# K and v of ten tiles as seven block products per pair, in a kernel for linear attention and routed experts

## The chip, the cores and the metric

The kernel runs on one core of one Trainium2 chip. The metric is the device time of one launch in microseconds. Engines are called as the profile calls them: PE multiplies matrices, DVE, ACT and POOL work on tiles in SBUF (DVE and ACT also in PSUM, where PE's results land), SP starts most transfers. Each engine takes its instructions in the order in which the program lists them.

## The reference

A sequence of 2048 rows of 512 numbers goes through two branches, which are mixed row by row by a sigmoid gate.

```
g = sigmoid((x * gate_w).sum(-1))
# branch A: linear attention, 32 heads of 16
q, k, v = split(x @ wqkv)
phi(y)  = concat(softmax(y @ w_phi), softmax(-(y @ w_phi)))   # 32 features a head
kv = sum over rows of phi(k)^T v ;  z = sum over rows of phi(k)
a  = (phi(q) kv) / (phi(q) z + 1e-6) @ wo
# branch B: for each of 32 heads the best of 16 x 16 experts
s1, s2 = x @ w_q @ k1, x @ w_q @ k2 ;  e = 16 * argmax(s1) + argmax(s2)
b  = sum over heads of gelu(x . u[e]) * v[e]
out = g * a + (1 - g) * b
```

## The kernel before

The rows are cut into 16 tiles of 128 (`t`). Each tile lies transposed, as four blocks of 128 x 128 (`k` = 0 to 3). All products keep float32 accuracy by three matmuls: every operand is held as a high part (`xh`, `wah`, `wbh`) and a low part (`xl`, `wal`, `wbl`, the source less the high part), and `mm3` adds high x high, high x low and low x high. A projection of one tile on 512 columns (`proj`) is 4 x 3 = 12 matmuls of 128 x 512 into one PSUM bank. Four banks rotate under the name `mm`, three under `tr`, one (`acc`) holds the sums over rows.

The first stage, about 128 us, prepares weights and builds the sums over rows. Its loop over `t` does, for each tile:

- `x_load(t + 3)`: SP starts a load of 256 KB into one of three buffers (`xr`); `x_split` makes the high part on ACT and the low part on DVE (L132, L133).
- `vproj(t)` projects on v (weights `wbh`, `wbl`), and ACT copies the result into `vs[t]`. `kproj(t)` projects on k (weights `wah`, `wal`, with `w_phi` folded in), and DVE takes differences from each head's maximum and minimum (`softmax_diffs`, four instructions: the differences of tile t). Tiles 14 and 15 get their v much later.
- ACT takes the exponential (L346), `ksoft` the sums and reciprocals on DVE (L200, L201) and the product with them on POOL (L202). The text calls these exp(t), sum(t) and k_mult(t).
- Every second tile `kvacc` adds phi(k)^T v of two tiles: 32 small matmuls a tile. Ones in a 17th column of v give the sums z; for tiles 14 and 15 `kvz` makes them alone with 32 matmuls of one column.
- By the table `plan`, `score_w` multiplies a piece of `w_q` (1 MB, two buffers) with the keys. After two pieces, `score_planes(j)` copies the result to `wpl`, and SP starts a transpose by DMA into `wtp`; `score_join(j)` copies it back (`wtj`), splits it into `sh` on ACT and `sl` on POOL. `wpl`, `wtp` and `wtj` have one buffer each.

After the loop, `fold_q` folds `w_phi` into the query weights (`rawq`, loaded in the loop), `front_s` and the rest begin the second stage, a loop over the tiles for all that remains; there, in its second round, v of tiles 14 and 15 is projected.

Nothing is scheduled automatically: each engine's order is the order of these calls.

Of the kernel before, what the change touches and what calls it, by code (L numbers as in the profile page):

```python
# [20 lines left out]
P = 128  # L21
# [14 lines left out]
def mix_kernel(ctx, tc, xT, wqT, wkT, wv, wphi, wo, wq, kk, ug, ev, cst, out):  # L36
# [28 lines left out]
    xh = per.tile([P, NT, NK, P], F32R, name="xh")  # L65
    xl = per.tile([P, NT, NK, P], F32R, name="xl")
# [7 lines left out]
    wbl = per.tile([P, NK, D], F32R, name="wbl")  # L74
    uh = per.tile([P, NK, NW], F32R, name="uh")
# [8 lines left out]
    def xs(t, k):  # L84
        return xh[:, t, k, :], xl[:, t, k, :]
# [30 lines left out]
    warm = w1.tile([P, 384], BF16, bufs=1, name="warm")  # L116
# [8 lines left out]
    def x_load(t):  # L125
        r = rawx[t] = wa_.tile([P, NK, P], F32, tag="xr", bufs=3, name=f"xr{t}")
        if t > 0:
            sp.dma_start(r, xT[t])

    def x_split(t, ks=slice(0, NK)):  # L130
        r = rawx[t]
        (dve.tensor_copy if t < 3 else act.copy)(xh[:, t, ks], r[:, ks])  # L132
        dve.tensor_tensor(xl[:, t, ks], r[:, ks], xh[:, t, ks], op=ALU.subtract)  # L133
# [33 lines left out]
    def fold_turn(tmp, wh, wl):  # L167
# [6 lines left out]
        for k in range(NK):  # L174
            act.copy(by_head(wh[:, k]), by_row(o[k]))
            dve.tensor_tensor(by_head(wl[:, k]), by_row(o[k]), by_head(wh[:, k]), op=ALU.subtract)

    acc = psum.tile([P, 512], F32, tag="acc", name="kvacc")[:, :8 * (F + 1)].rearrange("p (g c) -> p g c", c=F + 1)
    phis, vs, pvs, wsP, stk, joins = {}, {}, {}, {}, {}, []

    def vproj(t, ks=range(NK)):
        if ks[0] > 0:
            return proj(pvs.pop(t), t, wbh, wbl, 0, D, ks)
        pv = pvs[t] = mm_bank(f"pv{t}")
        proj(pv, t, wbh, wbl, 0, D, ks)
        v = vs[t] = home(t).tile([P, H, F + 1], F32, name=f"v{t}", tag="v")
        if t < NT - 2:
            pool.memset(v[:, :, F], 1.0)
        return lambda: act.copy(v[:, :, :F], pv.rearrange("p (h f) -> p h f", f=F))

    def kproj(t):
        pk = mm_bank(f"pk{t}")
        proj(pk, t, wah, wal, 0, D)
        phis[t] = home(t).tile([P, 1024], F32, tag="d", name=f"d{t}")
        stk[t] = w1.tile([P, 192], F32, tag="stt", name=f"st{t}")
        softmax_diffs(pk, phis[t], stk[t])

    def ksoft(t):
        d, st = phis[t], stk.pop(t)
        dve.tensor_reduce(st[:, 64:128], g64(d), axis=AX.X, op=ALU.add)  # L200
        dve.reciprocal(st[:, 128:192], st[:, 64:128])  # L201
        pool.tensor_tensor(g64(d), g64(d), b64(st[:, 128:192]), op=ALU.mult)  # L202

    def kvacc(t):
        n = F + 1 if t < NT - 2 else F
# [45 lines left out]
    pool.memset(warm, 0.0)  # L251
# [648 lines left out]
```

## Time and profile before

| | |
|---|---|
| time, median of 3 runs | 380.23 us (380.21 to 380.63) |
| the profiled execution, first to last instruction | 378.1 us |
| busy: PE, DVE, ACT, POOL | 99%, 84%, 62%, 41% |
| granted clock of PE | 1.000 |

A page of the profile gives busy time by engine, the chain of work that ended last, and groups of equal instructions as "line, engine, operation, written tile <- read tiles, shapes, count | busy us, mean ns | idle time before, and what ended it". Rows in order of time have start, duration, engine, line and tiles. PEld is PE's loading of weights, which overlaps its matmuls; SPq and ACTq are instructions that start transfers.

### The profile page before, as it was taken

Reading aid. Unit: us, or ns where it says so; the run is one execution under the profiler, and the core shown is the slowest. Engines: PE = TensorE matmul, PEld = TensorE weight load, DVE = VectorE, ACT = ScalarE, POOL = GpSimd, SP = SyncE. Lnnn points to the kernel's source line nnn. Section 1 sums busy time; section 2 is a strip of 40 time slices with the busy share of each in tenths; the row PEclk is TensorE's granted clock in tenths of the full one; section 3 lists DMA queues with packets and bytes.
Section 4 is the critical chain, followed back from the end, with each engine's and each line's share of the span. In section 5 each row is a group of like instructions: output and inputs, shape, how many; then the busy total and the mean of one; then the engine's idle time right before and its main releaser. Section 6 shows DMA issues by size and latency. Waiting matters only on the chain.

```text
span 378.1 us, 9073 instructions
## 1 busy us (share of the span) xinstructions
PE 372.5 (99%) x3613; PEld 294.3 (78%) x3613; DVE 315.9 (84%) x776; ACT 235.5 (62%) x420; POOL 154.9 (41%) x164
## 2 busy tenths in 40 slices
PE   8999999999999999999999999999999999999996
PEld 4766777777768888888878888888888888888775
DVE  4479866866868968879999999999999999999993
ACT  4436554644646345769668777696686686687741
POOL 1014435325325232946427335344454454364700
PEclk9999999999999999999999999999999999999999
DMA  7757878478592034242351452441532524523201
GB/s 272 307 187 259 258 218 237 157 222 237 188 305 84 3 85 83 73 83 76 80 99 49 105 84 57 85 100 32 121 62 65 127 56 72 126 52 77 64 34 57
DMA packets 72219, 46.69 MB, mean 123 GB/s; under 512 B 63600, under 2 KB 64496, under 8 KB 69872
## 3 DMA queue, kind: packets, MB, share of 16 engines
q1 hardware_dynamic: 71312, 45.24, 44.6%
q10 hardware_dynamic: 864, 0.87, 0.8%
q8 instruction: 28, 0.46, 0.5%
q14 instruction: 15, 0.12, 0.1%
HBM read 26.43 MB, written 4.19 MB: 81 GB/s over the span
## 4 chain that ended last, share of the span: by engine, by line
PE 97%; DMA 1%; ACT 0%; SPq 0%; DVE 0%; issue 0%; ACTq 0%; DVEq 0%
PE po L627 11%; PE s L56 8%; PE s L57 8%; PE s L58 8%; PE po L634 5%; PE pq L56 5%; PE pv L56 4%; PE pk L56 4%; PE ws L225 4%; PE pv L57 4%; PE pq L58 4%; PE pk L57 4%; PE pq L57 4%; PE pk L58 4%; PE pv L58 4%; PE oT L518 3%
## 5 line engine op out<-in xcount | busy, mean ns | idle before, releaser
L432 POOL TENSOR_TENSOR w<-d,zb 128x512 f32<-128x512 f32 x32 | 40.9, 1294 | 83.4 <-ACT d L426 81.1
L202 POOL TENSOR_TENSOR d<-d,st 128x1024 f32<-128x1024 f32 x16 | 31.0, 1935 | 74.4 <-DVE st L201 40.5
L56 PE MATMUL s<-sh,xh 128*128 128x512 f32 x128 | 51.0, 399 | 0.0
L57 PE MATMUL s<-sl,xh 128*128 128x512 f32 x128 | 49.9, 390 | 0.0
L58 PE MATMUL s<-sh,xl 128*128 128x512 f32 x128 | 49.8, 389 | 0.0
L426 ACT ACTIVATE d<-d 128x512 f32<-128x512 f32 x32 | 20.1, 632 | 38.0 <-DVE d L98 29.3
L467 POOL TENSOR_TENSOR d<-d,st 128x512 f32<-128x512 f32 x30 | 31.2, 1062 | 28.5 <-DVE st L461 25.6
L509 ACT COPY pt<-tp 128x1024 uint16<-128x1024 uint16 x28 | 36.4, 1369 | 1.0 <-PE kvacc L209 1.0
L346 ACT ACTIVATE d<-d 128x1024 f32<-128x1024 f32 x16 | 17.0, 1064 | 28.5 <-DVE d L100 28.5
L499 ACT COPY pl<-d 128x1024 uint16<-128x1024 uint16 x28 | 29.2, 1045 | 4.4 <-POOL d L467 4.4
L58 PEld LDWEIGHTS s<-sh,xl 128*128 128x128 f32 x128 | 24.0, 188 | 5.1
L56 PEld LDWEIGHTS s<-sh,xh 128*128 128x128 f32 x128 | 24.0, 188 | 4.7
L57 PEld LDWEIGHTS s<-sl,xh 128*128 128x128 f32 x128 | 24.1, 188 | 4.5
L56 PE MATMUL pq<-wah,xh 128*128 128x512 f32 x64 | 26.7, 418 | 0.0
L56 PE MATMUL pv<-wbh,xh 128*128 128x512 f32 x64 | 26.0, 407 | 0.0
L436 DVE TENSOR_REDUCE st<-d 128x32 f32<-128x512 f32 x32 | 21.7, 683 | 5.0 <-ACT d L426 3.5
L57 PE MATMUL pv<-wbl,xh 128*128 128x512 f32 x64 | 25.2, 394 | 0.3 <-DVE wbl L51 0.3
L200 DVE TENSOR_REDUCE st<-d 128x64 f32<-128x1024 f32 x16 | 19.5, 1218 | 7.0 <-ACT d L346 7.0
L56 PE MATMUL pk<-wah,xh 128*128 128x512 f32 x64 | 25.3, 396 | 0.0
L58 PE MATMUL pv<-wbh,xl 128*128 128x512 f32 x64 | 25.1, 392 | 0.0
L58 PE MATMUL pq<-wah,xl 128*128 128x512 f32 x64 | 25.1, 392 | 0.0
L57 PE MATMUL pk<-wal,xh 128*128 128x512 f32 x64 | 25.0, 391 | 0.0
(177 smaller groups left out, 1029.5 us busy)
## 6 DMA issues: line engine op xcount, KB each, us to landing
wq<-wq SPq DMA_DIRECT2D x16, 1024.0 KB, 6.0
xr<-xT SPq DMA_DIRECT2D x15, 256.0 KB, 6.0
y<-ot SPq DMA_DIRECT2D x15, 256.0 KB, 2.3
rawk<-wkT SPq DMA_DIRECT2D x1, 1024.0 KB, 6.1
rawq<-wqT SPq DMA_DIRECT2D x1, 1024.0 KB, 5.7
rawo<-wo SPq DMA_DIRECT2D x4, 256.0 KB, 3.8
rawu<-ug SPq DMA_DIRECT2D x2, 258.0 KB, 6.3
rawv<-wv ACTq DMA_DIRECT2D x2, 256.0 KB, 4.2
```

The source lines that it names most:

```text
L56: pe.matmul(o, ah, bh, start=(first and i == 0), stop=False)
L57: pe.matmul(o, ah, bl, start=False, stop=False)
L58: pe.matmul(o, al, bh, start=False, stop=(last and i == n - 1))
L200: dve.tensor_reduce(st[:, 64:128], g64(d), axis=AX.X, op=ALU.add)
L202: pool.tensor_tensor(g64(d), g64(d), b64(st[:, 128:192]), op=ALU.mult)
L426: act.activation(hs(d, i), hs(d, i), AF.Exp)
L432: pool.tensor_tensor(hs(e["w"], i), hs(e["ph"], i), hs(zb, i), op=ALU.mult)
L436: dve.tensor_reduce(pair(e["st"][:, 64:128])[:, :, i], hs(e["ph"], i), axis=AX.X, op=ALU.add)
L467: eng.tensor_tensor(g64(d)[:, gs_], g64(d)[:, gs_], r[:, gs_].unsqueeze(2).to_broadcast([P, 32, F]), op=ALU.mult)
L499: act.copy(pl, e["ph"][:, halves[i]].bitcast(U16).rearrange("p (c j) -> p j c", j=2))
L509: act.copy(p16[:, :, 4 * i:4 * i + 4, :], e["tp"][i].rearrange("p (j g) n -> p j g n", j=2))
L627: pe.matmul(po, a, b, start=(i == 0), stop=False)
```

## The change

Tiles 5 to 14 are taken in five pairs (t, n = t + 1). The rows of a pair, the two halves of the 512 inputs, and the columns of k and v form blocks of 2 x 2, and seven block products in the form of Strassen and Winograd replace eight. With A the x blocks and B the weight blocks (B11 and B21 of k, B12 and B22 of v):

- weight sums, once: t1 = B12 - B11, b3 = B22 - B12, t2 = b3 + B11, t4 = B21 - t2. They need an unsplit copy of the folded k weights (`kraw`), four 128x1024 subtractions or additions of POOL and their high parts on ACT near the start, and t4 a little later. They borrow the space of `eh`/`el` (b3), `uh`/`ul` (t2) and a quarter of `sh`/`sl` (t4) before these get their own contents.
- sums of x, per pair: `Sums.add` makes four 128x256 sums in place in the two load buffers on POOL, `Sums.high` two high parts on ACT (`gh`, and tile 15's `xh`), `Sums.low` two low parts on POOL (`gl`, and tile 15's `xl`).
- products (`prod`, 2 x 3 = 6 matmuls each): the banks `pk`, `pu`, `pv`, `pk` of a pair are a, b, c, d, and `pe` is e. Where a result is needed in two banks, ACT copies the finished bank into the next one and PE adds on top of that seed.
- v of both tiles is finished by two DVE additions; k's differences of the second tile (`behind`) move to the next pair.

`ksoft` falls into `k_sum` and `k_mult`. v of tile 14 is made in the loop, so kvz(14) and its late projection go. The splits of `u` and of half of `ev` move to POOL. x buffers become four; the split x is held in three pieces so that the unsplit weights can lie where tiles 11 to 14 come later.

```diff
+    dve.tensor_tensor(t2r, rawv[:, 2:4], rawv[:, 0:2], op=ALU.subtract)
+    act.copy(t1r, rawv[:, 0:2])
...
+    act.copy(eh, t2r)
+    dve.tensor_tensor(el, t2r, eh, op=ALU.subtract)
...
+    pool.tensor_tensor(t1r, t1r, kraw[:, 0:2], op=ALU.subtract)
+    pool.tensor_tensor(t2r, t2r, kraw[:, 0:2], op=ALU.add)
+    act.copy(t1h, t1r)
+    pool.tensor_tensor(t1l, t1r, t1h, op=ALU.subtract)
...
+        if t == 0:
+            act.copy(t2h, t2r)
+            pool.tensor_tensor(t2l, t2r, t2h, op=ALU.subtract)
+        k_mult(t)
+        if t == 2:
+            t4r = kraw[:, 2:4]
+            pool.tensor_tensor(t4r, t4r, t2r, op=ALU.subtract)
+            act.copy(t4h, by4(t4r))
+        for j, tp in score_old:
+            score_join(j, tp)
+    x_load(8)
+    Sums.add(5)
+    Sums.high(5)
+    Sums.low(5)
+    pool.tensor_tensor(t4l, by4(t4r), t4h, op=ALU.subtract)
+    x_high(7)
+    x_high(8)
...
+    for t in range(5, NT - 1, 2):
+        n = t + 1
+        for u in more:
+            x_load(u)
...
+        for u in (t + 2, t + 3):
+            if u < NT - 1:
+                x_low(u)
+        if behind:
+            k_diffs(behind)
+        prod(a, tile_of(t, 0), b11, True)
+        act.copy(b, a)
+        if t + 3 < NT:
+            Sums.add(t + 2)
+        if t < NT - 3:
+            join_all()
+        prod(e, sums(0, 2), b1, True)
+        prod(b, sums(1, 0), b2, False)
+        act.copy(c, b)
+        prod(a, tile_of(t, 2), b21, False)
+        k_diffs(t)
...
+        score(2)
+        if t == NT - 3:
+            rawq = stage(wqT, "rawq")
+        for u in (t - 3, t - 2):
+            if u > 2:
+                kvacc(u)
+        k_exp(t)
+        k_sum(t)
+        act.copy(vn, by16(e))
+        prod(b, sums(0, 0), b3, False)
+        act.copy(d, b)
+        prod(c, sums(1, 2), b22, False)
+        dve.tensor_tensor(vt, by16(c), vn, op=ALU.add)
+        dve.tensor_tensor(vn, by16(b), vn, op=ALU.add)
+        prod(o2, tile_of(n, 2), b4, False)
+        if t + 3 < NT:
+            Sums.high(t + 2)
+            Sums.low(t + 2)
...
+    x_split(t)
+    k_diffs(t - 1)
+    kproj(t)
+    k_exp(t - 1)
...
+    join_all()
+    fq = fold_q(rawq, wah, wal)
-    kvz(NT - 2)
+    kvacc(NT - 2)
```

How the instructions stand on POOL from the start to the first pair. Names carry the tile's number and a serial number (`d0` is the phi of tile 0, `xr6` the loaded tile 6, `sl` from `wtj1` the join of planes 1). Before:

```order
L202 TENSOR_TENSOR d0_281<-d0_281,st0_282 128x1024
L202 TENSOR_TENSOR d1_323<-d1_323,st1_324 128x1024
L242 TENSOR_TENSOR sl_68<-wtj0_335,sh_67 128x4x128
L202 TENSOR_TENSOR d2_354<-d2_354,st2_355 128x1024
L188 MEMSET v3_420 128x32
L202 TENSOR_TENSOR d3_436<-d3_436,st3_437 128x1024
```

The same stretch of POOL in the changed kernel, where `xraw1` holds t1 and t2, `ul` the low part of t2, and `xraw0` the unsplit k weights, later t4:

```order
L379 TENSOR_TENSOR xraw1_69<-xraw1_69,xraw0_66 128x1024
L380 TENSOR_TENSOR xraw1_69<-xraw1_69,xraw0_66 128x1024
L382 TENSOR_TENSOR t1l_80<-xraw1_69,t1h_79 128x1024
L426 TENSOR_TENSOR ul_84<-xraw1_69,uh_83 128x1024
L275 TENSOR_TENSOR d0_299<-d0_299,st0_300 128x1024
L275 TENSOR_TENSOR d1_343<-d1_343,st1_344 128x1024
L315 TENSOR_TENSOR sl_72<-wtj0_355,sh_71 128x4x128
L275 TENSOR_TENSOR d2_374<-d2_374,st2_375 128x1024
L430 TENSOR_TENSOR xraw0_66<-xraw0_66,xraw1_69 128x1024
L245 MEMSET v3_442 128x32
L275 TENSOR_TENSOR d3_458<-d3_458,st3_459 128x1024
```

Four 128x1024 instructions stand ahead of tile 0's k_mult, and one behind tile 2's. Further on, from tile 4's k_mult to the low parts of the first pair's sums, POOL has in the changed kernel:

```order
L275 TENSOR_TENSOR d4_511<-d4_511,st4_512 128x1024
L315 TENSOR_TENSOR sl_72<-wtj1_604,sh_71 128x4x128
L175 TENSOR_TENSOR xr6_427<-xr6_427 128x256
L176 TENSOR_TENSOR xr6_427<-xr5_359,xr6_427 128x256
L177 TENSOR_TENSOR xr5_359<-xr6_427,xr5_359 128x256
L178 TENSOR_TENSOR xr5_359<-xr5_359 128x256
L188 TENSOR_TENSOR gl_82<-xr6_427,gh_81 128x512
L188 TENSOR_TENSOR xl15_70<-xr5_359,xh15_67 128x512
```

Seven of these eight come between tile 4's k_mult and the operands of the pair's second and third product. On ACT, from tile 2's exponential to tile 4's, the changed kernel has one instruction more, the copy from `xraw0` (t4h), behind tile 2's exponential:

```order
L266 ACTIVATE d2_374<-d2_374 128x1024
L432 CAST sh_71<-xraw0_66 128x4x256
L254 COPY v3_442<-pv3_429 128x32x16
L303 COPY wpl1_470<-ws1_380 128x1024
L152 CAST xh0_65<-xr5_359 128x512
L266 ACTIVATE d3_458<-d3_458 128x1024
L254 COPY v4_495<-pv4_482 128x32x16
L303 COPY wpl2_530<-ws2_517 128x1024
L152 CAST xh0_65<-xr6_427 128x512
L266 ACTIVATE d4_511<-d4_511 128x1024
```

All other rows of this piece stand in the same order as before. On SP, at the end of the first stage, before:

```order
L122 DMA wq15_1196<-wq 128x2048
L232 DMA_TRANSPOSE wtp6_1200<-wpl6_1198 128x8x128
L299 DMA rawu1_1202<-ug 128x516
L122 DMA rawq_1314<-wqT 128x2048
L299 DMA rawe0_1316<-ev 128x512
L299 DMA rawe1_1329<-ev 128x512
L232 DMA_TRANSPOSE wtp7_1359<-wpl7_1357 128x8x128
```

And in the changed kernel:

```order
L143 DMA wq15_1186<-wq 128x2048
L305 DMA_TRANSPOSE wtp6_1190<-wpl6_1188 128x8x128
L386 DMA rawu1_1291<-ug 128x516
L386 DMA rawe0_1293<-ev 128x512
L305 DMA_TRANSPOSE wtp7_1352<-wpl7_1350 128x8x128
L143 DMA rawq_1354<-wqT 128x2048
L386 DMA rawe1_1453<-ev 128x512
```

The transpose of planes 7 moves ahead of the load of `rawq`.

More of the change, by code (lines that the diff above doesn't have):

```diff
@@ L74, in mix_kernel @@
     wbl = per.tile([P, NK, D], F32R, name="wbl")
+    t1h = per.tile([P, 2, D], F32R, name="t1h")
+    t1l = per.tile([P, 2, D], F32R, name="t1l")
+    gh = per.tile([P, NK, P], F32R, name="gh")
+    gl = per.tile([P, NK, P], F32R, name="gl")
     uh = per.tile([P, NK, NW], F32R, name="uh")
@@ L331, in mix_kernel @@
                     kvacc(u)
[L332 removed]
+        if t > 0:
             x_split(t + 2)
[L334 to L346 removed]
@@ L356, in mix_kernel @@
+    front_s(0, 1)
+    for k in range(2):
+        act.copy(eh[:, k, :], rawe[k])
+    next(fq)
+    k_exp(t)
+    k_sum(t)
+    for k in range(2):
+        pool.tensor_tensor(el[:, k, :], rawe[k], eh[:, k, :], op=ALU.subtract)
+    k_mult(t)
     ca.close()
```

242 lines of the change are left out of this document (161 added, 81 removed).

## The prediction

> **What bounds the kernel now.** I read the page's engine totals and chain first, then the stretches of 10 us, then the chain in order of time for the loop over tiles.
>
> ```profile
> PE 372.5 (99%) x3613; PEld 294.3 (78%) x3613; DVE 315.9 (84%) x776; ACT 235.5 (62%) x420; POOL 154.9 (41%) x164
> PE 97%; DMA 1%; ACT 0%; SPq 0%; DVE 0%; issue 0%; ACTq 0%; DVEq 0%
> 70.00:80.00 10.00, 10.00 (x176) 7.26 (x175) 6.20 (x10) 5.13 (x8) 5.31 (x5) 1.00 0.75 224
> ```
>
> The first row is busy time, the second the chain that ended last, the third one stretch of the loop over tiles (columns: stretch, its length, then PE, PEld, DVE, ACT and POOL busy, clock, DMA share, GB/s). PE is busy for the whole stretch and the chain is 97% PE. So every matmul taken out shortens the run by its issue interval, and every gap put into PE lengthens it, since there is hardly a gap today in which it could hide. In that stretch DVE is free for 3.8 us of 10, POOL for 4.7, ACT for 4.9: room for new work, if it comes at the right time.
>
> ```profile
> 42.67 1.85 PE ws L225 x16
> 44.52 1.14 PE kvacc L209 x79
> 45.65 0.43 PE pv L56
> ...
> 56.80 1.85 PE ws L225 x16
> 127.26 0.55 PE kvacc L217 x33
> ```
>
> One pair of tiles lasts 56.80 - 42.67 = 14.13 us: 1.85 for the score weights, 1.14 for two kvacc, 11.14 for 48 projection matmuls, 0.232 each.
>
> **What goes.** Seven products of 6 matmuls replace 48: 6 x 0.232 = 1.39 us per pair, 5 pairs, **6.96 us**; a pair would last 12.74. The 32 one-column matmuls of kvz(14) go too, **0.55 us**. Projecting v14 and its kvacc earlier moves work within PE and saves nothing.
>
> **What comes.** Prices of one instruction, from the groups by form:
>
> ```profile
> L202 POOL TENSOR_TENSOR d<-d,st 128x1024 f32<-128x1024 f32 x16 | 31.0, 1935 | 74.4 <-DVE st L201 40.5 <-ACT sh L241 26.3 <-ACT wtj L237 7.6
> L404 POOL TENSOR_TENSOR px<-x,px 128x256 f32<-128x256 f32 x16 | 11.8, 740 | 0.0
> L242 POOL TENSOR_TENSOR sl<-wtj,sh 128x512 fp32r<-128x512 f32 x8 | 10.3, 1286 | 2.1 <-ACT sh L241 2.1
> L346 ACT ACTIVATE d<-d 128x1024 f32<-128x1024 f32 x16 | 17.0, 1064 | 28.5 <-DVE d L100 28.5
> L189 ACT COPY v<-pv 128x512 f32<-128x512 f32 x16 | 9.4, 586 | 11.0 <-PE pv L58 11.0
> L230 ACT COPY wpl<-ws 128x1024 uint16<-128x1024 uint16 x8 | 8.1, 1012 | 12.8 <-PE ws L225 12.6 <-ACT uh L50 0.2
> L132 ACT CAST xh<-xr 128x512 fp32r<-128x512 f32 x13 | 8.1, 622 | 0.0
> L237 ACT COPY wtj<-wtp 128x1024 uint16<-128x1024 uint16 x8 | 10.8, 1346 | 0.7 <-DMA wtp<-wpl 0.7
> L241 ACT CAST sh<-wtj 128x512 fp32r<-128x512 f32 x8 | 5.0, 620 | 0.3
> L200 DVE TENSOR_REDUCE st<-d 128x64 f32<-128x1024 f32 x16 | 19.5, 1218 | 7.0 <-ACT d L346 7.0
> L201 DVE RECIPROCAL st<-st 128x64 f32<-128x64 f32 x16 | 8.8, 553 | 0.5
> L98 DVE TENSOR_TENSOR d<-pk,st 128x512 f32<-128x512 f32 x16 | 10.9, 681 | 0.0
> L133 DVE TENSOR_TENSOR xl<-xr,xh 128x512 fp32r<-128x512 f32 x15 | 11.3, 752 | 4.5 <-ACT xh L132 4.4
> ```
>
> A 128x1024 POOL subtraction of two whole operands isn't in the trace. Between L202 (1.94, second operand broadcast) and twice L242 (2.57) I take 0.74 + 3 x 0.55 = 2.40, the line through L404 and L242. A PSUM-to-PSUM copy on ACT isn't there either: from 0 to twice L189; L189's 0.59 is the nearest row.
>
> In a running pair the new work fits. POOL: four additions (2.96), two low parts (2.57), two k_mult (3.87), one sl (1.29), memsets: 11.0 of 12.74. ACT: near 10. DVE: 8 x 0.68 of differences, 2 x 1.77 of sums, two v additions at 0.68, two x_low at 0.75: 11.8. The seeds (b from a, c from b, d from b) are each covered by another product of 1.39 us that stands between on PE, so PE waits for none while ACT is on time; without that cover each would cost 0.59 and its start. Sums for the next pair start a pair ahead, so gl and xl15 are ready at the second and third product. The running pairs cost nothing extra, then.
>
> Small edits that I take at nothing: t1r's copy, t2r, eh and el near the start lie where ACT and DVE wait for loads and for PE today (if that room were gone, the fold's copies would be late by el's 1.5, two L133); the splits of u and of ev move from DVE to POOL, behind work that PE doesn't wait for; the warm matmuls read another zeroed tile; a fourth xr buffer only lets loads start earlier.
>
> The trouble lies where a queue gets new work in front of old: three places.
>
> **Place 1, kvacc(0).**
>
> ```profile
> 17.06 2.06 ACT L175 CAST wah<-turnk 128x512 fp32r<-128x512 f32 x4 [2.21 <-PE turnk L171]
> 21.25 0.69 DVE L94 TENSOR_REDUCE st<-pk 128x32 f32<-128x512 f32 x1 [1.08 <-PE pk L58]
> 23.05 0.68 DVE L100 TENSOR_TENSOR d<-st,pk 128x512 f32<-128x512 f32 x1
> 27.09 1.94 POOL L202 TENSOR_TENSOR d<-d,st 128x1024 f32<-128x1024 f32 x1 [14.54 <-DVE st L201]
> 29.58 0.76 PE L209 MATMUL kvacc<-v,d 128*32 128x17 f32 x64
> ```
>
> Today k_mult(0) ends at 29.03 and kvacc(0) starts at 29.58: 0.55 us of slack. POOL now has four 128x1024 subtractions (t1r, t2r, t1l, t2l) ahead of k_mult(0). The first needs the raw k weights, copied after 19.1 on ACT: start 20.2. Then 20.2 + 4 x 2.40 = 29.8, + 1.94 = 31.7. **PE waits 2.1 us** (3.3 with 2.57 apiece plus waits on ACT's t1h and t2h; 0.3 with 1.94).
>
> **Place 2, the sums of pair (5, 6).** kvacc(2) ended at 45.66 and now ends at T = 47.7; the second product needs gl, the low part of a sum of x.
>
> ```profile
> 37.96 1.94 POOL L202 TENSOR_TENSOR d<-d,st 128x1024 f32<-128x1024 f32 x1 [2.44 <-DVE st L201]
> 40.16 1.06 ACT L346 ACTIVATE d<-d 128x1024 f32<-128x1024 f32 x1 [1.56 <-DVE d L100]
> DMA to landing us min/median/max: 2.8/7.3/8.1
> ```
>
> The first row is k_mult(2), ending at 39.9; the second exp(3); the third the transposed score planes (wtp). Now POOL makes t4r after k_mult(2), till 42.3, and ACT's copy t4h, which waits for it, stands ahead of v3, wpl1, xh5 and exp(3): t4h 43.4, v3 44.0, wpl1 45.0, xh5 45.6, exp(3) 46.7, over five later than now. DVE: sum(3) 48.4, differences(4) 50.9 (2.48 us, 21.25 to 23.73 above). ACT's wpl2 has one buffer and waits until the transpose of wpl1 lands, 45.0 + 7.3 = 52.3: wpl2 53.3, xh6 53.9, exp(4) 55.0. Then sum(4) 56.8, k_mult(4) 58.7, sl1 60.0, four additions 63.0, gl 64.3. PE has run six matmuls and two of the next by T + 1.9 = 49.6: **it waits 14.7 us**. If the transpose lands in 2.8, exp(4) goes by DVE from 50.9 and gl is at 61.3: 11.7. What PE does after this (b's seed, behind xh8 and so behind x8's load; c's seed behind sh2) is ready about as each product before it ends.
>
> **Place 3, rawq.**
>
> ```profile
> 108.90 0.33 SPq L122 DMA_DIRECT2D rawq<-wqT  x1
> 115.19 1.25 SPq L232 DMA_TRANSPOSE wtp<-wpl  x1
> 111.43 1.31 ACT L50 CAST uh<-rawu 128x258 fp32r<-128x258 f32 x4
> 113.81 1.36 ACT L237 COPY wtj<-wtp 128x1024 uint16<-128x1024 uint16 x1
> 116.80 1.99 PE L148 MATMUL foldq<-wp,rawq 32*128 32x32 f32 x64
> rawq<-wqT SPq DMA_DIRECT2D x1, 1024.0 KB, 5.7
> ```
>
> The transpose of planes 7 needs the one wtp buffer, so it starts only when the copy of planes 6 is done (113.81 + 1.36 = 115.17; start 115.19). Today rawq is ahead of it on SP; in the changed kernel behind. Counted from the end E of the loop's last product: product c ended at -1.4, the two v additions on DVE take till 0, xl15 till 0.8, the differences of tile 14 till 3.3, exp(14) till 4.4, the four uh copies till 5.8, the copy of planes 6 till 7.2, the transpose's issue till 8.4, and rawq lands at 14.1. kproj(15) needs xl15 at its third matmul, 0.35 after it could have it, and ends at E + 3.1 (12 matmuls). **PE waits 0.35 + 11.0 us**, 10 to 12.5 by the DMA's spread. The join of planes 7 lands by E + 15.3 at the latest and ends some 3.3 later (1.35 + 0.62 + 1.29), before front_s(0,1) needs it at about E + 22: no fourth wait.
>
> **The clock after a wait.**
>
> ```profile
> 1.21 5.15 PE L270 MATMUL warm<-warm 128*128 128x384 bf16 x16 [1.21 <-POOL tab L253]
> ```
>
> Out of rest, 16 matmuls of 384 columns took 5.15 us; at 0.232 per 512 columns it would be 2.8. So PE loses 2.4 us when it starts from rest. For each of the two long waits I take 2.0, since PE pauses again behind them; 0 to 2.4. **4 us.** The Trainium skill ("TensorE: Matmul & The Clock Gate", Part 1: The HAM clock gate) says that PE's clock is halved after an idle window of about 3.4 us and restored after as much sustained work; by it, an estimate, each wait would cost 1.7, the sum 0.6 less. The row agrees in kind; no row here shows a long wait in mid-run.
>
> **The sum.** The span is 378.1, the median of the runs 380.23; the 2.1 around it stay. 380.23 - 6.96 - 0.55 + 2.1 + 14.7 + 11.35 + 4.0 = **404.9 us**, chance 0.54.
>
> **Rivals.**
> 1. The three waits, but full clock after them: 400.9. For: the rest before the first matmuls may have been much longer than 11 us, and the granted clock in the stretches stands at 1.00 even so. Against: the row above has PE at half pace from rest, and 11 us are 47 missing matmuls. 0.24.
> 2. DVE becomes the bound of the pairs:
>
> ```profile
> 34.24 1.29 POOL L242 TENSOR_TENSOR sl<-wtj,sh 128x512 fp32r<-128x512 f32 x1
> 34.44 1.64 DVE L133 TENSOR_TENSOR xl<-xr,xh 128x512 fp32r<-128x512 f32 x1
> ```
>
> An x_low (0.75 on average) took 1.64 while POOL's subtraction ran. With POOL 86% busy both x_low of a pair may pay 0.9 more: 11.8 + 1.8 = 13.6 against 12.74, 0.9 x 5 = 4.5 on top: 409.4. Against: vector instructions overlap by some 0.08, 20 of them, so the pair just fits. 0.08. The Trainium skill ("SBUF — State Buffer", Who interferes with whom) says that a vector instruction with two SBUF inputs and a POOL instruction that reads SBUF shut each other out for a whole instruction; these two rows agree.
> 3. rawq isn't held up, or lands before kproj(15) ends: 404.9 - 11 - 2 = 391.9. Against: SP took its rows in order above. 0.08.
> 4. Faster: the queues keep up. It decides at gl: if it is written by T + 1.9, and the other two waits stay under the 7.5 saved; with none, 372.7. For: half of POOL and a third of DVE is free. Against: POOL alone has 1.94 + 1.29 + 2.96 + 1.29 = 7.5 us between sum(4) and gl, and sum(4) ends after kvacc(2) already today:
>
> ```profile
> 48.41 0.55 DVE L201 RECIPROCAL st<-st 128x64 f32<-128x64 f32 x1
> ```
>
> 48.96 against 45.66. So gl would be 10.8 us behind T even without t4r and wpl2. 0.05.
> 5. The change does nothing, its gain and its waits equal: 0.01.
>
> **Range.** 394 to 411. The low bounds of all three places at full clock give 372.7 + 0.3 + 11.7 + 10.35 = 395.1; the top is rival 2 with place 1 at 3.3, 410.6. Rivals 3 to 5 lie outside, 0.14. A measurement of this kernel can tell about 0.2%, 0.8 us, from no change. Faster 0.05, same 0.01, slower 0.94.
>
> **What would show it.** Right: PE idle for about 2 us ahead of kvacc(0), released by k_mult on POOL; for 12 to 15 ahead of the second product of pair (5, 6), released by gl on POOL; for about 11 ahead of foldq, released by rawq's DMA; pairs of 12.7 us between; and matmuls right after the two long gaps at twice the interval. Wrong: PE at 10.0 of 10 in the stretches from 45 to 75 us; rawq issued before E; pairs over 13.5 us; the late stage, which is not edited but for v14, changing by more than the 3 us of that.

## The result and the profile after

| | time, median (range) | runs | ratio to before, 95% interval |
|---|---|---|---|
| before | 380.28 us (380.21 to 380.63) | 4 | |
| changed kernel | 409.94 us (409.04 to 411.03) | 4 | 1.0772 (1.0746 to 1.0798) |

The changed kernel is slower by 29.7 us, and the forecast of 404.9 with its range of 394 to 411 holds the time. The profiled execution lasts 407.8 us (before 378.1), at a mean granted clock of 0.958 (before 1.000).

The page of the changed kernel: busy time of PE and PEld, the chain that ended last, and PE and its clock in 40 slices of 10.2 us.

```profile
PE 375.5 (92%) x3519; PEld 294.2 (72%) x3519; DVE 331.9 (81%) x782; ACT 253.1 (62%) x449; POOL 202.4 (50%) x206
PE 73%; DVE 9%; ACT 7%; POOL 4%; issue 3%; DMA 3%; SPq 0%; ACTq 0%; POOLq 0%; DVEq 0%
PE   8998909999998099989999999999999999999996
PEclk9998966999999669998999999999999999999999
```

The chain was 97% PE and is 73%: DVE, ACT, POOL and DMA have come into it. PE has two holes, and in each of them and right behind it the clock is at 0.6. PE is busy for 3 us more with less to do, because matmuls at half clock take longer.

The timeline of PE in the changed kernel at the three places of the prediction, in order of time:

```profile
32.24 0.74 PE L282 MATMUL kvacc<-v,d 128*32 128x17 f32 x64 [1.79 <-POOL d L275]
61.07 0.79 PE L446 MATMUL pe<-t1h,gh 128*128 128x512 f32 x1 [9.59 <-ACT gh L183]
63.28 0.80 PE L446 MATMUL pe<-t1h,gl 128*128 128x512 f32 x1 [0.99 <-POOL gl L188]
129.95 0.50 PE L58 MATMUL pk<-wah,xl 128*128 128x512 f32 x1 [1.25 <-DVE xl L156]
142.61 3.64 PE L207 MATMUL foldq<-wp,rawq 32*128 32x32 f32 x64 [10.09 <-DMA rawq<-wqT]
```

Each of the three waits is there. They last 1.8, 10.6 and 11.3 us, the second and third in two parts. Place 1 is released by k_mult(0) on POOL and place 3 by xl15 and rawq's DMA, as named. At place 2 the prediction had named gl on POOL, but PE stood first and longest at gh on ACT, the high part of the same sum; gl held it for the last 1.0 us.

PE's clock in three stretches of the changed kernel (stretch, length, then PE, PEld, DVE, ACT, POOL busy, clock, DMA share, GB/s):

```profile
34.00:36.00 2.00, 2.00 (x6) 1.52 (x5) 2.00 (x4) 0.42 (x1) 1.39 (x1) 0.50 0.88 352
64.00:66.00 2.00, 2.00 (x6) 1.54 (x5) 2.00 (x2) 1.97 (x3) 2.00 (x2) 0.50 0.63 174
142.00:150.00 8.00, 7.39 (x74) 6.55 (x75) 0.00 (x0) 0.63 (x2) 3.29 (x3) 0.54 0.09 32
```

PE works without a break there, at half the clock. Behind the long waits that was forecast; behind the wait of 1.8 us it was not.

The pairs, by the start of the score weights in each:

```profile
69.03 1.92 PE L298 MATMUL ws<-wq,kp 128*32 128x512 f32 x16
81.19 1.92 PE L298 MATMUL ws<-wq,kp 128*32 128x512 f32 x16
94.24 1.92 PE L298 MATMUL ws<-wq,kp 128*32 128x512 f32 x16
108.15 1.92 PE L298 MATMUL ws<-wq,kp 128*32 128x512 f32 x16
120.88 1.92 PE L298 MATMUL ws<-wq,kp 128*32 128x512 f32 x16
```

12.16, 13.05, 13.91 and 12.73 us. The first has one kvacc less (0.57), so its share of the forecast is 12.17. The saving of 1.39 a pair is real, and 1.5 us in all are lost in the second and third pair. The third has a wait of 0.79 us for d's seed in it. In the first five runs below, which leave the pairs as they are, it took 12.75 four times and 13.15 once.

The late stage, which the prediction expected to get shorter by v14's 3.35 us (12 x 0.232 and a kvacc of 0.57). First the starts of the query projections of tiles 1 and 2 in the kernel before, then the same in the changed kernel, with a wait between them:

```profile
142.24 0.39 PE L56 MATMUL pq<-wah,xh 128*128 128x512 f32 x1
160.05 0.50 PE L56 MATMUL pq<-wah,xh 128*128 128x512 f32 x1
```

```profile
171.82 0.39 PE L56 MATMUL pq<-wah,xh 128*128 128x512 f32 x1
182.46 0.74 PE L282 MATMUL kvacc<-v,d 128*32 128x16 f32 x64 [1.98 <-ACT v L254]
189.71 0.50 PE L56 MATMUL pq<-wah,xh 128*128 128x512 f32 x1
```

That round took 17.81 us with v14's matmuls and 17.89 without. A new wait stands in their place, with half clock behind it. The clock isn't why the round got no shorter: in the run with rawq early below, PE kept full clock behind the same wait of 2.0 us, then stood 0.83 us for kvb, the copied sums over rows, and the round took 17.80.

### The profile page after: what moved, and what is told of

It is laid out like the page before. It is cut to its first block, busy times and chain, and to the rows that moved or that the text cites. A ratio compares the mean times of both kernels' runs of the same rounds, so it can differ in the third digit from the quotient of the medians.

```text
span 407.8 us, 8985 instructions
## 1 busy us (share of the span) xinstructions
PE 375.5 (92%) x3519; PEld 294.2 (72%) x3519; DVE 331.9 (81%) x782; ACT 253.1 (62%) x449; POOL 202.4 (50%) x206
## 4 chain that ended last, share of the span: by engine, by line
PE 73%; DVE 9%; ACT 7%; POOL 4%; issue 3%; DMA 3%; SPq 0%; ACTq 0%; POOLq 0%; DVEq 0%
PE po L817 10%; PE s L56 8%; PE s L57 7%; PE s L58 7%; PE po L824 5%; PE pq L56 4%; PE pq L58 4%; PE pq L57 4%; PE pk L446 3%; PE oT L708 2%; PE pu L446 2%; DVE xl L156 2%; PE pp L57 2%; PE pp L58 2%; PE pp L56 2%
## 5 line engine op out<-in xcount | busy, mean ns | idle before, releaser
L56 PE MATMUL s<-sh,xh 128*128 128x512 f32 x128 | 52.3, 408 | 0.0
L57 PE MATMUL s<-sl,xh 128*128 128x512 f32 x128 | 51.1, 399 | 0.0
L58 PE MATMUL s<-sh,xl 128*128 128x512 f32 x128 | 51.0, 398 | 0.0
L275 POOL TENSOR_TENSOR d<-d,st 128x1024 f32<-128x1024 f32 x16 | 32.3, 2020 | 37.2 <-DVE st L271 25.2
L156 DVE TENSOR_TENSOR xl<-xr,xh 128x512 fp32r<-128x512 f32 (+2 forms) x17 | 23.2, 1380 | 12.4 <-ACT xh L152 12.3
L57 PE MATMUL pq<-wal,xh 128*128 128x512 f32 x64 | 25.0, 390 | 0.0
L266 ACT ACTIVATE d<-d 128x1024 f32<-128x1024 f32 x16 | 17.0, 1062 | 12.2 <-DVE d L121 12.2
L817 PE MATMUL po<-wbh,xh 128*128 128x512 f32 x60 | 24.0, 400 | 0.0
L817 PE MATMUL po<-wbl,xh 128*128 128x512 f32 x60 | 23.4, 390 | 0.0
L666 DVE TENSOR_TENSOR eq<-s,mx 128x512 bf16<-128x512 f32 x32 | 22.1, 692 | 1.2
```

The costliest lines, as they stand in the source:

```text
L56: pe.matmul(o, ah, bh, start=(first and i == 0), stop=False)
L57: pe.matmul(o, ah, bl, start=False, stop=False)
L58: pe.matmul(o, al, bh, start=False, stop=(last and i == n - 1))
L156: dve.tensor_tensor(l[:, ks], rawx[t][:, ks], h[:, ks], op=ALU.subtract)
L666: dve.tensor_tensor(e["eq"][:, 512 * half:512 * half + 512].rearrange("p (h f) -> p h f", f=F), p3, mx.unsqueeze(2).to_broadcast([P, H, F] ...
L817: pe.matmul(po, a, b, start=(i == 0), stop=False)
```

## The experiments

Each kernel was run against the kernel before on the same chip; times are medians.

**The load of rawq moved back ahead of the transpose.**

```diff
             load_wq()
+            if done == 15:
+                rawq = stage(wqT, "rawq")
             if done % 2 == 0:
                 score_planes(done // 2 - 1)
```

> One edit to the changed kernel (409.94 us): the load of rawq is started as soon as 15 pieces of the score weights are done, so on SP it stands ahead of the transpose of planes 7, as in the kernel before. Theory A, the order on SP makes the 10.1 us wait ahead of foldq: that wait goes, and with it the 3.2 us that foldq and front_s(0,0) lose to the half clock behind it. Next late is the join of planes 7, whose low part was written at 142.8 in the changed kernel, where front_s(0,1) could then start at about 140.7: a new wait of about 2 us and up to 1.5 us of clock. Time 398 to 402. Theory B, the 1 MB transfer itself is late (too much traffic, or no buffer free before): the load starts earlier but lands as late, 408 to 411.

Measured: 400.06 us (398.35 to 401.10), ratio 1.0505 (1.0463 to 1.0546). SP and PE in it:

```profile
121.89 0.33 SPq L143 DMA_DIRECT2D rawq<-wqT  x1
132.34 1.99 PE L207 MATMUL foldq<-wp,rawq 32*128 32x32 f32 x64
141.47 0.50 PE L56 MATMUL s<-sh,xh 128*128 128x512 f32 x1 [1.09 <-ACT sh L314]
142.82 0.50 PE L57 MATMUL s<-sl,xh 128*128 128x512 f32 x1 [0.85 <-POOL sl L315]
```

Theory A holds in every part: rawq starts at 121.89, not 137.63, foldq waits for nothing and takes 1.99 us and not 3.64, and the forecast next-late work, the join of planes 7, costs 1.9 us of waits. One line in the wrong place of a queue was worth 10 us.

**The sums of the first pair moved ahead.**

```diff
         if t == 4: (behind the split of x6, ahead of exp(4))
+            Sums.add(5); Sums.high(5); Sums.low(5)
-    t4r, t4h behind k_mult(2)
+    t4r behind the loop, x_high(7), x_high(8), then t4h, t4l
```

> One edit to the changed kernel (409.94 us): the four additions for the sums of x of pair (5, 6), their high parts and low parts stand right behind the split of tile 6, ahead of exp(4), k_mult(4) and the last join, and t4r with its high part t4h comes behind them instead of behind k_mult(2). Theory A, queue order makes the 10.6 us of waits at gh and gl: without t4h in its way exp(3) runs at about 43 instead of 47.4, the additions start at about 49 and gl is there at about 54 instead of 63.2. The two waits shrink to about 3 us in all, and the clock loss behind them from 2.3 to about 1.3; 400 to 404. Theory B, the ten running pairs of the loop are held by DVE, POOL or the buffers of x anyway, so that what PE gains ahead of pair (5, 6) it loses behind it: over 406.

Measured: 409.64 us (408.99 to 411.41), ratio 1.0769 (1.0735 to 1.0802). PE's longest wait there, and ACT ahead of it:

```profile
63.99 0.80 PE L446 MATMUL pu<-uh,xh 128*128 128x512 f32 x1 [7.74 <-ACT pu L474]
60.15 0.62 ACT L152 CAST xh<-xr 128x512 fp32r<-128x512 f32 x1 [3.24 <-DMA xr<-xT]
62.41 1.04 ACT L440 CAST sh<-xraw 128x1024 fp32r<-128x1024 f32 x1 [1.64 <-POOL xraw L436]
63.36 0.58 ACT L474 COPY pu<-pk 128x512 f32<-128x512 f32 x1
```

The waits for gh and gl shrank from 10.6 to 3.5 us as theory A had it, but the gain is nil and the time is theory B's: b's seed stands on ACT behind the high part of x8, whose load had just been started, and behind t4h, which waits for POOL. So the wait moved one product on. The prediction had called this seed "ready about as each product before it ends", which held only as long as gh was later.

**k_mult(0) moved ahead of t1l and t2l.**

```diff
-    pool.tensor_tensor(t1l, t1r, t1h, op=ALU.subtract)
...
-            pool.tensor_tensor(t2l, t2r, t2h, op=ALU.subtract)
         k_mult(t)
+        if t == 0:
+            pool.tensor_tensor(t1l, t1r, t1h, op=ALU.subtract)
+            pool.tensor_tensor(t2l, t2r, t2h, op=ALU.subtract)
```

> One edit to the changed kernel (409.94 us): k_mult(0) stands ahead of t1l and t2l on POOL (t1r and t2r stay ahead of it), so two of the four 128x1024 subtractions are out of its way. The wait of 1.8 us ahead of kvacc(0) goes in any case. Theory A, the waits at the three places add, as the prediction summed them: that wait and the 1.6 us of half clock behind it are gained, 406 to 407. Theory B, the sums of pair (5, 6) are set by a chain of DVE, ACT and POOL that doesn't hang on PE (differences, exponentials, t4r, k_mult), so the wait at gh grows by what is gained here: 409 to 411.

Measured: 410.50 us (409.02 to 411.34), ratio 1.0780 (1.0748 to 1.0811). PE's two longest waits in this kernel up to product e, then the second of them in the run with rawq early, which has place 1 as it was:

```profile
33.13 0.50 PE L58 MATMUL pv<-wbh,xl 128*128 128x512 f32 x1 [1.38 <-DVE xl L156]
61.54 0.80 PE L447 MATMUL pe<-t1h,gh 128*128 128x512 f32 x1 [11.78 <-ACT gh L183]
```

```profile
61.63 0.80 PE L448 MATMUL pe<-t1h,gh 128*128 128x512 f32 x1 [11.55 <-ACT gh L183]
```

Theory B. The wait ahead of kvacc(0) is gone, one of 1.4 us for xl3 has come just behind its place, and the wait for gh is 11.8 us and not 9.6. The longer wait isn't this edit's alone: with rawq early PE still waited 1.8 us ahead of kvacc(0), but kept full clock behind it, came earlier too and waited 11.6. Both show that gh's time is set by other engines. In the five kernels that leave those queues as they are (the changed kernel, rawq early, this one, v15 first and the filled waits), product e starts between 61.07 and 61.63 us, whenever PE arrives. Waits of PE in series that end at the same foreign queue don't add.

**v15 copied ahead of the exponentials.**

```diff
+        if a == 1:
+            v15()
         gelu_act(a)
         soft_exp(a)
-        if a == 1:
-            v15()
```

> One edit to the changed kernel (409.94 us): in the second round of the late stage ACT copies v15 out of PSUM ahead of the tanh and the exponentials of tile 1, no longer behind them. In the changed kernel PE waited 1.98 us for this copy ahead of kvacc(15) (the projection of v14, which lay in that gap before, is gone), and the granted clock was 0.92 and 0.91 in the 20 us around it, 1.7 us. Theory A, this wait is why the late stage got no shorter although 3.3 us of matmuls left it: 406 to 408. Theory B, DVE (9.56 of 10 us busy there) sets the pace of that round: 409 to 411.

Measured: 413.14 us (411.06 to 413.98), ratio 1.0845 (1.0808 to 1.0882). PE and ACT of this kernel in the same round:

```profile
188.21 1.22 PE L708 MATMUL oT<-pt,kvb 64*32 64x128 f32 x32 [2.92 <-ACT kvb L847]
187.64 1.07 ACT L847 COPY kvb<-kvacc 32x128 f32<-32x128 f32 x4
```

The wait for v15 went, and one of 2.9 us for kvb came. Neither theory had this: the end of the round is set by a chain through DVE, POOL and ACT (the coefficients, their planes, then kvb), which is nearly as long as PE's work was. In this execution the second round took 17.78 us, as before, and the third, with half clock behind the new wait, 16.46 for 14.85. That covers its span of 409.0, which is 1.2 longer; the median is 3 us worse, and why the other runs are slower still is open.

**Matmuls put into the two long waits.** They write banks that are overwritten behind them; nothing else changes.

```diff
+        for _ in range(42):   # ahead of foldq
+            pe.matmul(o[0], xs(0, 0)[0], wbh[:, 0, :], start=True, stop=True, skip_group_check=True)
...
+        for _ in range(40 if t == 5 else 0):   # ahead of product e
+            pe.matmul(e, xs(0, 0)[0], wbh[:, 0, :], start=True, stop=True, skip_group_check=True)
```

> The changed kernel (409.94 us) with matmuls that nobody reads put into its two long waits: 40 of 512 columns between the first and the second product of pair (5, 6) (9.3 us at 0.232 each, in a wait of 9.6) and 42 ahead of foldq (9.7 us in a wait of 10.1). The queues of all other engines are as they were, so the waits for gh and for rawq end when they ended. Theory A, PE runs at half clock behind a long wait because it stood idle: it stays at full clock, foldq's first half takes 2.0 us and not 3.6, front_s(0,0) 2.9 and not 4.4, products e and b of pair (5, 6) 1.4 each; 5 us less in all, 404 to 406. Theory B, the clock falls there for another reason (a stretch of the program, or the load of the other engines): 409 to 411.

Measured: 409.04 us (408.51 to 409.39), ratio 1.0747 (1.0731 to 1.0763). The fold and a stretch behind it, then a stretch behind the 1.8 us wait ahead of kvacc(0), which is untouched here:

```profile
142.17 1.99 PE L209 MATMUL foldq<-wp,rawq 32*128 32x32 f32 x64 [0.46 <-DMA rawq<-wqT]
144.00:146.00 2.00, 2.00 (x13) 1.57 (x10) 0.00 (x0) 0.00 (x0) 1.06 (x1) 0.54 0.00 0
...
34.00:36.00 2.00, 2.00 (x10) 1.66 (x9) 2.00 (x5) 0.00 (x0) 1.60 (x1) 1.00 0.74 291
```

Theory A is half right, and the time is theory B's. With PE kept busy, foldq runs at full speed (1.99). But behind the 0.46 us that were left of the wait, and the fold's 64 small matmuls, the clock fell to 0.54 all the same, two microseconds later; at place 2 it fell behind the 3.8 us that were left. So at most 0.9 us came back, and the intervals of the two ratios overlap. The last row shows chance at work: the same wait of 1.8 us between small matmuls was followed by half clock in two of five profiled executions (the changed kernel and the run with v15 first), and by full clock in three (this one, rawq early, sums first).

**All queues ahead of the first pair reordered**, with rawq early and k_mult(0) first.

```diff
+        if t == 4: x_load(8)
+        t == 1: t4r behind the join of planes 0;  t == 3: t4h behind wpl1
+        t == 3: x_split(5), x_split(6), Sums.add(5) ahead of k_mult(3)
+        t == 4: join of planes 1, Sums.high(5), Sums.low(5), sl, k_mult(3), then score(2)
+    in pair 5: b's seed, t4l, k_mult(4), x_split(7), x_split(8); planes 2 joined behind c's seed
```

> The changed kernel with rawq early (400.06 us in the first set) and k_mult(0) ahead of t1l and t2l, and the queues ahead of pair (5, 6) put into another order: x6 split and its sums made at tile 3 ahead of k_mult(3); the high parts and low parts of the sums right behind the join of planes 1, ahead of wpl2; x8 loaded with x7; t4r on POOL behind the join of planes 0, t4h on ACT behind wpl1, t4l inside pair 5; the seed of b ahead of the splits of x7 and x8; planes 2 joined behind the seed of c. Theory A, the 12.6 us of waits at place 2 are queue order alone, no engine lacks time: the waits at gh, gl and b's seed shrink to 0 to 2 us and 2 to 3 us of half clock go with them; 384 to 389. Theory B, behind the order stands a lack of time on POOL or DVE between tiles 2 and 8 (as the prediction's fourth rival argued: 7.5 us of POOL work between sum(4) and gl): at least half of the waits comes back at later products or in the pairs (7, 8) and (9, 10); 393 to 400.

Measured: 387.53 us (386.64 to 388.36), ratio 1.0180 (1.0162 to 1.0199). PE's longest wait in the pairs:

```profile
61.40 0.50 PE L457 MATMUL pk<-sh,xh 128*128 128x512 f32 x1 [2.04 <-ACT pk L518]
```

Theory A, 12.5 us less than with rawq early alone. Place 2 was order, not lack of time; 2 us of it are left at d's seed. Which of the moves did how much was not taken apart.

**The end of the loop and the late stage reordered too.**

```diff
+    pair 13: wtj of planes 6 copied early; x_split(15) ahead of the additions for v
+    behind the loop: sh, sl of planes 6, join of planes 7, then exp(14) and u
+    late, second round: v15 ahead of the exponentials, kv_final ahead of c_planes
```

> As the kernel with the queues ahead of pair (5, 6) in another order, and besides: in the last pair planes 6 are copied out of the transpose's buffer at the usual place (so that the transpose of planes 7 can start), their split comes behind the last product, ahead of exp(14) and the copies of u, with the join of planes 7 behind it; x15 is split ahead of the last two additions for v; in the second round of the late stage v15 is copied ahead of the exponentials and kvb ahead of the planes of the coefficients. Theory A: the waits at xl15 (1.2) and at the planes of front_s(0,1) (1.9) go, with 1.7 us of clock behind them, and about 1.5 us in the late stage; 5 us less than the kernel it builds on, 379 to 384, near the kernel before (380.5). If nothing were lost anywhere the sum is 372.7 and some 3 us of v14 in the late stage that DVE keeps: 376. Theory B, DVE sets the end of the loop and the late stage: 384 or more.

Measured: 382.49 us (381.48 to 383.66), ratio 1.0050 (1.0033 to 1.0066). DVE and ACT ahead of d's seed in pair (5, 6); then the late stage's second and third round (pq of tiles 1, 2, 3):

```profile
52.01 4.96 DVE L156 TENSOR_TENSOR xl<-xr,xh 128x512 fp32r<-128x512 f32 x2
59.40 1.06 ACT L266 ACTIVATE d<-d 128x1024 f32<-128x1024 f32 x1 [0.71 <-DVE d L121]
60.83 0.59 ACT L524 COPY pk<-pu 128x512 f32<-128x512 f32 x1
...
145.85 0.39 PE L56 MATMUL pq<-wah,xh 128*128 128x512 f32 x1
161.07 0.50 PE L56 MATMUL pq<-wah,xh 128*128 128x512 f32 x1
178.07 0.50 PE L56 MATMUL pq<-wah,xh 128*128 128x512 f32 x1
```

Within A's range. Two x_low beside a POOL that was busy from 51.70 to 58.78 took 2.48 us each, and through the differences and exp(5) they held d's seed. The Trainium skill ("SBUF — State Buffer", Who interferes with whom) has an instruction of DVE with two SBUF inputs contend with a POOL instruction that reads SBUF; the row agrees, 2.48 us against the 0.75 on average in the kernel before. In the late stage the second round fell from 17.89 to 15.22, and the third rose from 14.85 to 17.00: the stage as a whole took 250.0 us.

**d's seed ahead of exp(t) in every pair; x3 split earlier.**

```diff
-        k_exp(t); k_sum(t)
         act.copy(d, b)
+        k_exp(t); k_sum(t)
...
+        if t == 1:
+            x_split(3)
         k_diffs(t)
```

> As the kernel with all orders changed (382.49 us), with two more changes of order: in every pair ACT seeds d ahead of exp(t), which waits for DVE's differences behind two slow x_low (4.96 us for both in pair (5, 6), beside POOL); and x3 is split ahead of the differences of tile 1, so that its low part no longer runs beside t1l (2.72 us there) and no longer makes PE wait 1.35 us in v3's projection. Theory A, the rest of the loss up to the late stage is these waits: 2.1 + 0.8 us for d's seed with about 2 us of half clock, and 1.35 for xl3; 5 to 6.5 us less, 376 to 378, faster than the kernel before (380.5). Theory B, DVE is the bound of the pairs (two x_low slowed by POOL, 11.8 us of other work in 12.75): pairs stay at 13 us or more on average and the time at 380 to 382.

Measured: 383.13 us (382.06 to 384.38), ratio 1.0074 (1.0053 to 1.0095); no gain over the last kernel, and above both ranges. The waits for d's seed and xl3 went and the profiled execution has a clock of 1.000, but the pairs took 13.5 us on average, as theory B had it. This came:

```profile
64.45 0.50 PE L462 MATMUL pe<-t1h,gl 128*128 128x512 f32 x1 [1.90 <-POOL gl L188]
61.77 1.28 POOL L318 TENSOR_TENSOR sl<-wtj,sh 128x512 fp32r<-128x512 f32 x1
63.12 1.27 POOL L188 TENSOR_TENSOR gl<-xr,gh 128x512 fp32r<-128x512 f32 x1
```

**The casts of wo behind the copy of the numerators.**

```diff
+        if a == 2:   (behind mid_num(0), instead of at the end of a == 1)
+            wbh, wbl of blocks 2 and 3
```

> As the kernel with d's seed first, and one more order: in the late stage the casts of the last two blocks of wo on ACT, which wait for their DMA, stand behind the copy of tile 0's numerators (xh) and not ahead of it. Theory A, the stage from the first query projection to the end (250.4 us before, 250.5 in the changed kernel, 250.0 with all orders changed) is held by DVE, whose next work there (low part of the numerators, differences of tile 2) waits 2.1 us for this copy; so it gets 1 to 2 us shorter. Theory B, another chain sets it (POOL's low parts of wo, the transposes): 0, or up to 0.5 longer.

Measured: 383.45 us (382.75 to 384.73), ratio 1.0086 (1.0067 to 1.0106). Theory B: the late stage took 249.95 us against 249.85, and PE now waits for the weights instead:

```profile
165.33 0.50 PE L844 MATMUL po<-wbl,xh 128*128 128x512 f32 x1 [0.64 <-POOL wbl L925]
```

**POOL: the low parts of the sums ahead of the join and of both k_mult.**

```diff
             Sums.high(t + 2); Sums.low(t + 2)
+        (the join's low part); k_mult(behind or 4)
         k_mult(t)
+    x_split(15) ahead of exp(13); wo's loads and casts earlier; b's first seed ahead of exp(4)
```

> As the kernel with d's seed first (383.13 us; its own profiled span 380.5), and: on POOL the low parts of the next pair's sums stand ahead of the join's low part and of both k_mult, in every pair, and k_mult(4) behind those of pair (7, 8); b's first seed ahead of exp(4); x15 split ahead of exp(13); in the late stage wo's first two blocks are split right behind v15's copy, the last two loaded right behind that and cast ahead of the planes, and tile 0's product with wo takes wo's low parts last. Theory A, what is left is order: PE's waits for gl (1.9 and 0.34, the pairs at 14.81 and 13.72 us where others take 12.75) were POOL's k_mult and sl ahead of gl; third round of the late stage 16.9 us where before it took 14.84, by waits for wo. Gains 3.0 in the pairs, 0.5 and 0.8 at the edges, 1.5 to 2 late: 377 to 379, faster than the kernel before (380.3). Theory B, POOL has no time between 43 and 68 us (about 23 us of work there) whatever the order, so the wait moves to the next user (k_mult, adds): the first two pairs together still take 27 us or more; 380 to 383.

Measured: 381.67 us (381.07 to 385.50), ratio 1.0034 (1.0015 to 1.0054), the lowest median of all, and still 0.3% above the kernel before. PE, DVE and POOL in pair (7, 8):

```profile
69.08 0.74 PE L282 MATMUL kvacc<-v,d 128*32 128x17 f32 x64 [0.60 <-POOL d L275]
67.16 0.69 DVE L115 TENSOR_REDUCE st<-pk 128x32 f32<-128x512 f32 x1 [1.83 <-POOL d L275]
74.18 1.30 POOL L188 TENSOR_TENSOR gl<-xr,gh 128x512 fp32r<-128x512 f32 x1 [1.86 <-ACT gh L183]
```

Theory B in its number, 13.4 to 13.8 us a pair, but not in its reason. POOL waits 1.9 us of each pair for ACT's gh, DVE 1.8 for POOL's k_mult, PE 0.6 for the same. No engine is full (PE is busy for 13.1 of 13.7 us, DVE for 11.7, POOL for 11.6); a ring of waits through three queues has become longer than PE's 12.74. This is read off the trace, and no run took the ring apart.

**gl first, then both k_mult, then the other low parts.**

```diff
             Sums.high(t + 2)
+            Sums.low(t + 2, 0)
+        k_mult(behind or 4); k_mult(t)
+            Sums.low(t + 2, 1); (the join's low part)
+    b's first seed ahead of exp(4); x_split(15) ahead of exp(13)
+    differences(15) ahead of sum(14); sum(15), k_mult(15) behind the selections of tile 0
```

> As the kernel with d's seed first (383.13 us), the late stage as there, and: on POOL in every pair first gl of the next pair, then both k_mult, then the second low part and the join's; b's first seed ahead of exp(4); x15 split ahead of exp(13); at the end of the loop DVE takes the differences of tile 15 ahead of sum(14), and sum(15) behind the two selections of front_s(0), so that the transpose for the masks of tile 0 (for which PE waited 1.56 us in the kernel with POOL's order changed) starts earlier. Theory A: pairs of 12.2 to 12.9 us, query projection of tile 0 at 125.5 to 127 us (130.65 with d's seed first, 127.74 in the kernel before), late stage 250; 377.5 to 379.5, faster than the kernel before. Theory B, POOL and DVE together have no more room in a pair of 12.75 us (each x_low beside POOL 1.3 to 2.4 us and not 0.7): pairs stay at 13.3 to 13.8, as with POOL's order changed, and the time at 380.5 to 382.

Measured: 404.48 us (404.31 to 404.71), ratio 1.0625 (1.0602 to 1.0648). Neither theory; 25 us above A's range, with PE's first wait of this kind:

```profile
67.83 0.79 PE L467 MATMUL pu<-uh,xl 128*128 128x512 f32 x1 [4.00 <-POOL xl L188]
```

The second low part is read by product b already (`sums(1, 0)`), which I had overlooked. This one instruction, 1.3 to 1.7 us long, behind two k_mult made PE wait 13.7 us in four pairs, with half clock behind the waits. Another 2.8 us went to k_mult(15), moved in the same run.

**That mended, the join behind the exponential, exp(t) behind gh.**

```diff
+            Sums.low(t + 2); k_mult(behind or 4); k_mult(t); (the join's low part)
+        ACT: exp(behind), join, wpl, copy of e, d's seed, gh, exp(t)
```

> The last kernel's order corrected: the second low part of the sums is needed by product b at its third matmul already, not first by c. On POOL in every pair now: additions, gl, the second low part, both k_mult, the join's low part. On ACT: both seeds, exp of the tile before, then the join, the score planes, the copy of e, d's seed, gh, and only then exp(t). X15 split ahead of exp(13), the differences of tile 15 ahead of sum(14); the late stage as in the kernel with d's seed first. Theory A: the 13.7 us of waits for the second low part go with the clock loss behind them, no new wait comes, pairs of 12.2 to 13.0 us, tile 0's query projection at 126 to 127.5 us, late stage 250 to 251: 378 to 380, at or below the kernel before (380.5). Theory B, DVE and POOL shut each other out so much that pairs stay at 13.3 to 13.8: tile 0's query projection at 128 to 130, 380.5 to 382.5.

Measured: 387.34 us (387.04 to 387.93), ratio 1.0174 (1.0151 to 1.0197). Neither: from the second on, pairs of 15.4 to 16.6 us.

```profile
69.46 1.06 ACT L266 ACTIVATE d<-d 128x1024 f32<-128x1024 f32 x1 [4.23 <-DVE d L121]
74.38 0.50 PE L467 MATMUL pk<-sh,xh 128*128 128x512 f32 x1 [2.50 <-ACT pk L529]
```

ACT sat 4.2 us behind the differences, which stood behind two slow x_low, with the join and d's seed queued behind it on ACT.

## Why the prediction was right, term by term

The balance of the profiled executions, from 378.1 to 407.8:

| term | forecast, us | measured, us |
|---|---|---|
| matmuls that go | -7.5 | -7.5 |
| place 1, kvacc(0) | +2.1 | +1.8 |
| place 2, gh and gl | +14.7 | +10.6 |
| place 3, xl15 and rawq | +11.35 | +11.3 |
| half clock | +4.0 | +7.1 |
| running pairs | 0 | +1.5 |
| late stage, v14: 3.35 come into the loop and should leave here | 0 | +3.4 |
| start | 0 | +0.7 |
| sum | +24.65 | +28.9 of 29.7 |

The sum is luck in part. Place 2 was put 4.1 us too high, and the clock, the pairs, v14 and the start together 8.7 too low; 0.8 us stay unexplained. The time lies near the top of the range, and not for the reason that the range's top was built on (rival 2).

**Places 1 and 3** came out in size, releaser and order, though xl15 was 1.25 us of place 3 and not 0.35; place 3 is shown by the run with rawq early. **Place 1** cost its 1.8 us in the sum but was worth nothing alone, since the waits for xl3 and gh took it up. The prediction's sum survives this because it had worked out gl's time from the queues and PE's arrival with place 1 in it.

**Place 2** was mis-sized in the step on the transpose: I took a landing of 7.3 us and named 11.7 for one of 2.8. It landed 3.2 us after its issue, so DVE's differences set exp(4), as the lower branch has it, and gl was written at 13.4 us after T (61.94 + 1.29 - 49.83), forecast 13.6. So gl came as forecast, and the wait was 1.1 us shorter than that branch's 11.7: PE stood for gh first, and two matmuls of product e ran at half clock before it stood for gl. That queue order was the cause is shown by the reordered kernel. The fourth rival's argument, that POOL's work between sum(4) and gl would hold gl in any case, holds for the order as it was only, since the additions could be moved ahead of that work.

**The clock** was put 3.1 us too low. Behind place 2 products e and b lost 2.3 us, behind place 3 foldq and front_s(0,0) 3.2 (3.64 for 1.99, and 4.4 for 2.9), where I had 2.0 each from a start out of rest; and place 1 lost 1.6, where I had none. Like the wait ahead of it, that 1.6 was taken up by place 2, where PE waited for gh in any case. Rival 1, full clock behind the waits, is out.

**Pairs**: "cost nothing extra" is nearly right for the order as it was changed, 12.2 to 13.05 and 12.75. The 13.91, over the 13.5 that the prediction had as a sign of being wrong, is this execution's alone. Rival 2 named a real mechanism, x_low slowed by POOL, and put its price too high here. The group of all x_low in the changed kernel:

```profile
L156 DVE TENSOR_TENSOR xl<-xr,xh 128x512 fp32r<-128x512 f32 x15 | 22.3, 1507 | 12.4 <-ACT xh L152 12.3
```

1.51 us on average, twice the 0.75 before. In the changed kernel PE felt little of it; with all orders changed it is what held exp(5) and d's seed.

**v14** was the step that failed in kind: "moves work within PE and saves nothing". It moved 3.35 us into a stage bound by PE out of one that chains through other engines hold nearly as tightly. Before, PE, full for the whole round, hid that; with v14 gone PE waits for v15, and with that mended for kvb, for the numerators, for wo. From tile 0's query projection to the end the stage took 250.4 us before, 250.5 in the changed kernel, and 249.85 to 254.3 in the twelve others, whatever was reordered. So the change saves 7.5 us and gives 3.4 back in a place that the prediction had left out. That the stage didn't shorten is measured; which chain would have to be shortened for it is open.

**The start** was taken at nothing: the first score weights began at 21.82 us, before at 21.14, and in the runs below at 21.4 to 22.3, always later. PE waits there for the first casts of v's weights; why these are later is open.

That leaves the question where Strassen's gain is in the best kernel, 381.67 us. Its trace has tile 0's query projection at 128.70 us, where the matmul count gives 127.74 - 7.5 + 3.35 = 123.6. The four pairs between the score weights took 54.5 us for 50.4 forecast, and the late stage 252.5 for 247.05. So the longer pairs and the first rounds of the late stage eat it. Whether an order exists that wins is open; seven of them didn't.

## What to carry to other kernels

Taking matmuls away from a kernel at 99% PE pays only as far as every product's operands come in time from engines that get more to do. List, for each new instruction, what stands behind it on its queue and which product reads that first; one instruction of 1.3 us in the wrong place made PE wait 13.7 us here. Waits in series that end at the same foreign queue share one price, so work out the time at which that queue delivers, and expect the next-late operand to take over when you mend the first. Moving work of one engine between stages is free only if that engine alone binds both.

## What the runs showed of the hardware

Half clock does not need a long wait. A wait of 1.8 us among small matmuls was followed by a granted clock of 0.50 in two of five executions, and one of 0.46 us with the fold's small matmuls behind it by 0.54. Small matmuls around the wait aren't needed either. In the last run PE waited three times for d's seed, with at least six matmuls of 512 columns on both sides: 2.50, 1.94 and 1.96 us. Behind the first two the clock stayed at 1.00; behind the third it fell:

```profile
105.30 0.50 PE L467 MATMUL pk<-sh,xh 128*128 128x512 f32 x1 [1.96 <-ACT pk L529]
108.00:110.00 2.00, 2.00 (x6) 1.58 (x5) 1.79 (x4) 0.43 (x1) 2.00 (x2) 0.50 0.53 157
```

So neither the length of a wait nor the size of the matmuls around it decides alone. The Trainium skill ("TensorE: Matmul & The Clock Gate", Part 1: The HAM clock gate) has the clock fall after an idle window of about 3.4 us and lets that window run free of the kernel's start; the chance from wait to wait fits the second, while the short waits are below the first. What makes the clock fall behind a short wait is open.
